# An adaLN transformer block on one core: first modulation in two column halves, E by V in 64x32 tiles, five equal score sets

## The chip, the core and the metric

The kernel runs on one core of a Trainium2 chip. The metric is the device time of one execution in microseconds. Three runs of the kernel before took 323.96, 324.77 and 324.98 us (median 324.77). Beside the times there is one profiled execution, whose trace gives start and duration of every instruction of the engines: PE (matrix engine, with PEld for its weight loads), DVE (vector), ACT (scalar), POOL (GpSimd) and SP, which here only starts transfers.

## The reference

One block of a transformer with adaptive layer norm, for 2048 tokens of width D = 640. A condition vector `c` gives six vectors of length 640, shift, scale and gate for each of two halves of the block.

```python
mod = (silu(c) @ w_mod).reshape(1, 6, 1, 640)        # sa, ca, ga, sb, cb, gb
h = layernorm(x) * (1 + ca) + sa
x = x + ga * attention(h)                            # 32 heads of 20, window of 256 keys, causal
h = layernorm(x) * (1 + cb) + sb
x = x + gb * ((sigmoid(h @ w_gate) * (h @ w_up)) @ w_down)   # inner width 1536
```

Attention: q, k and v are `h @ wqkv`; a query sees itself and the 255 keys before it; softmax over the scores times 20**-0.5; then `@ wo`.

## The kernel before

The 2048 tokens are worked on in eight chunks of 256 (`a` = 0 to 7), each of two blocks of 128 (`bi`). All weights lie in SBUF after the first quarter of the kernel. For every chunk:

- `ln1` (line 897): load, statistics on DVE (line 793), the power -1/2 on POOL (lines 800 and 802), scaling of the block (line 815), turning to columns-by-tokens (PE for chunks 0 and 1, a transposing DMA after that), and the modulation by shift and scale (line 839 and near).
- `qkv` (line 936): Q, K and V projections on PE, five steps of 128 rows each, 320 columns at a time. Each result is copied out of PSUM by ACT or DVE. Q and K are then turned again so that a head's 20 elements lie on partitions: four heads side by side, at partitions 0, 32, 64 and 96. This is done on PE (`NPQ` = 2: chunks 0 and 1) or by a transposing DMA (`transp_dma`).
- `attention` (line 1187): for each half `q` of the heads (16 heads) a chunk sees four blocks of keys. The scores of 16 heads come in sets of 128 x 2048 in PSUM. There is one PSUM tile for a set (`p_S`, four banks), so ACT must have taken the exponential of one set (1.88 us) before PE writes the next. In chunks 1 to 7 there are four main sets (`main_set`, 64-key by 32-row tiles, eight side by side) and one set for the ends of the window (`ends_set`, 128-key tiles, four side by side). POOL zeroes what lies outside the window with affine selections: four for a main set, two for an ends set. Chunk 0 has three sets (`score_set`).
- `burst` (line 1119): E by V for the 16 heads, in 128x32 tiles: all 128 keys of a block at a time, four heads side by side. V has two columns of ones beside each head, so the sum for the softmax comes with the product. The burst of one half is issued in front of the second score set of the next half (`AFTER` = 1), as one operation with it. `norm` then turns the result on DVE, divides and turns back.
- `outproj` and `mlp`: projection by `wo`, residual, second layer norm, gate and up projections, tanh on ACT, product on DVE, down projection, residual, store.

The small products take PSUM from a pool of four banks (`p_M`), shared by all projections, bursts and turnings; a bank is free again once ACT or DVE has read it.

The start is a stage of its own. The weights of the first modulation (`wm0`, 640 x 1280) come in five transfers of 128 rows; five groups of ten 64-column matmuls (`fnA`) follow their arrival, with filler matmuls between (`fill`) and one copy into `mA` (line 778) at the end, for which every modulation of chunk 0 (lines 831 and 832) waits. The first projection is Q of block 0.

The order of all engines is fixed ahead. `PLAN` is a list of 2097 codes, one for each operation: the operation's number times five plus its engine (0 PE, 1 ACT, 2 DVE, 3 POOL, 4 SP). Each engine issues its operations in that order; `schedule` only derives buffers, and `emit` the semaphore waits. Operations that may go to one of several engines (copies out of PSUM, modulations, scalings) have theirs from the list. All matmuls but the smallest are issued from one helper, lines 698 (whole array) and 699 (tiles).

Of the kernel before, what the change touches and what calls it, by code (L numbers as in the profile page):

```python
# [8 lines left out]
ALU = mybir.AluOpType  # L9
# [351 lines left out]
def c_pe(n):  # L361
# [114 lines left out]
]  # L476
NPH = 2
NPQ = 2
PQ = ()
KEEP = 3  # L480
DSAFE = 0.2
# [13 lines left out]
FILL = 1  # L495
WSE = (("dve", "pool"), ("dve", "pool"))
QMAX = 4.5
NE = 6
EW = 2048
PAIR = 0  # L500
PAIRO = 0
# [4 lines left out]
def build(nc, A_x, A_wqkv, A_wo, B_x, B_w_gate, B_w_up, B_w_down, c, w_mod, out, S=2048):  # L506
# [260 lines left out]
    for kt in range(NDT):  # L767
# [7 lines left out]
        if kt:  # L775
            fills.append(fill(FILL, oA[-1:]))
# [611 lines left out]
```

## Time and profile before

| | |
|---|---|
| runs | 323.96, 324.77, 324.98 us |
| span of the profiled execution | 321.8 us, 11465 instructions |
| its own time | not listed apart from the runs; their median is 3.0 us above the span |
| PE busy | 315.6 us (98%), 5045 matmuls |
| PEld busy | 236.8 us (74%) |
| ACT busy | 213.9 us (66%) |
| DVE busy | 198.8 us (62%) |
| POOL busy | 189.5 us (59%) |

Busy times are unions: overlapping matmuls count once, and a matmul's listed duration holds its way through the array, so a group's mean is longer than the distance from one matmul to the next. The chain of waits goes back from the last instruction to what released each step. In its rows a count such as x64 is the number of merged instructions.

### The profile page before, as it was taken

What the parts mean: (1) busy time and instruction counts of PE and PEld (TensorE: products, weight loads), DVE (VectorE), ACT (ScalarE), POOL (GpSimd) and SP (SyncE); (2) the same over time, 40 slices, a digit from 0 to 9 for tenths busy, and PEclk for the clock granted to TensorE, in tenths of its full rate; (3) what the DMA queues carried; (4) which work ended last, traced back from release to release, by engine and by line L of the source; (5) the groups of instructions that cost most, each with busy time, mean ns of one, the idle gap of its engine ahead of it and who ended that gap; (6) DMA issues with size and microseconds to landing.
All of it is one profiled execution on the core that took longest, in us unless ns stands there. A gap on an engine that the chain in (4) does not pass through costs nothing.

```text
span 321.8 us, 11465 instructions
## 1 busy us (share of the span) xinstructions
PE 315.6 (98%) x5045; PEld 236.8 (74%) x5045; DVE 198.8 (62%) x424; ACT 213.9 (66%) x229; POOL 189.5 (59%) x349
## 2 busy tenths in 40 slices
PE   6999999999999999999999999999999999999996
PEld 2677767677877777766777677877877777877885
DVE  4689987877886746584555555465534474386323
ACT  2699997877787986768686867676976746411220
POOL 3338759878768493949484848577575826601000
PEclk9999999999999999999999999999999999999999
DMA  7999999999922534126526100220800004002101
GB/s 249 348 262 278 223 179 248 194 225 295 206 36 43 88 75 55 44 63 108 77 19 111 37 22 2 63 42 25 132 18 4 22 22 104 20 5 61 43 0 41
DMA packets 62123, 32.92 MB, mean 102 GB/s; under 512 B 45946, under 2 KB 60794, under 8 KB 62074
## 3 DMA queue, kind: packets, MB, share of 16 engines
q1 hardware_dynamic: 59904, 29.73, 43.5%
q10 hardware_dynamic: 2170, 2.46, 2.8%
q8 instruction: 39, 0.64, 0.9%
q14 instruction: 10, 0.08, 0.1%
HBM read 18.68 MB, written 2.62 MB: 66 GB/s over the span
## 4 chain that ended last, share of the span: by engine, by line
PE 96%; DMA 1%; DVE 1%; ACT 1%; issue 0%; ACTq 0%
PE M L698 79%; PE S L699 8%; PE M L699 7%; DMA x<-in_A_x_dram 1%; ACT hT L831 1%; DVE st L793 1%; PE S L698 1%; PE S L690 0%; ACT stg L914 0%; ACTq L584 0%; DVE x L815 0%; DVE st L795 0%; ACT hT L914 0%; DVE x L1308 0%; DVE mA L778 0%
## 5 line engine op out<-in xcount | busy, mean ns | idle before, releaser
L1067 ACT ACTIVATE E<-S 128x2048 bf16<-128x2048 f32 x56 | 105.0, 1875 | 40.6 <-PE S L699 40.2
L1072 POOL TENSOR_SCALAR_AFFINE_SELECT E<-E 128x256 bf16<-128x256 bf16 x112 | 46.6, 427 | 57.1 <-ACT E L1067 25.1
L1076 POOL TENSOR_SCALAR_AFFINE_SELECT E<-E 128x512 bf16<-128x512 bf16 x112 | 70.6, 646 | 4.6 <-DVE x L815 1.2
L698 PE MATMUL M<-h2T,wg 128*128 128x256 bf16 x480 | 67.0, 273 | 0.0
L698 PE MATMUL M<-h2T,wu 128*128 128x256 bf16 x480 | 66.7, 273 | 0.0
L1289 DVE SCALAR_TENSOR_TENSOR hh<-sig,M 128x512 bf16<-128x512 f32 x48 | 32.4, 678 | 42.9 <-ACT sig L1287 26.4
L698 PE MATMUL M<-wd,hh 128*128 128x320 bf16 (+2 forms) x396 | 57.1, 295 | 0.0
L698 PEld LDWEIGHTS M<-h2T,wg 128*128 128x128 bf16 x480 | 45.4, 98 | 7.8 <-DVE T L1162 0.2
L698 PEld LDWEIGHTS M<-h2T,wu 128*128 128x128 bf16 x480 | 45.2, 98 | 7.3
L1287 ACT ACTIVATE sig<-M 128x512 f32<-128x512 f32 x48 | 28.5, 595 | 31.2 <-PE M L698 30.9
L698 PEld LDWEIGHTS M<-wd,hh 128*128 128x128 bf16 x396 | 37.2, 98 | 13.7 <-DVE hh L1289 0.2
L1045 POOL TENSOR_SCALAR_AFFINE_SELECT E<-E 128x1024 bf16<-128x1024 bf16 x28 | 32.0, 1147 | 4.9 <-ACT E L1041 3.4
L699 PEld LDWEIGHTS S<-QT,KT 20*64 20x64 bf16 (+1 forms) x1856 | 20.0, 100 | 17.4 <-issue 9.7
L699 PE MATMUL S<-QT,KT 20*64 20x256 bf16 (+5 forms) x1856 | 32.3, 228 | 0.4 <-issue 0.4
L1041 ACT ACTIVATE E<-S 128x2048 bf16<-128x2048 f32 x14 | 26.3, 1876 | 6.8 <-PE S L699 6.7
L793 DVE BATCH_NORM_STATS2 st<-x 128x6 f32<-128x320 bf16 x64 | 28.9, 479 | 2.4 <-DMA x<-in_A_x_dram 1.8
L1162 DVE STREAM_TRANSPOSE T<-M 128x512 f32<-128x512 f32 x32 | 21.5, 700 | 12.9 <-PE S L699 11.6
L698 PE MATMUL M<-wk,hT 128*128 128x320 bf16 x160 | 27.9, 299 | 0.0
L1308 DVE TENSOR_TENSOR x<-M,x 128x320 bf16<-128x320 f32 (+2 forms) x33 | 15.4, 475 | 18.8 <-PE M L698 18.6
L698 PE MATMUL M<-wq,hT 128*128 128x320 bf16 x160 | 26.2, 299 | 0.7 <-DVE hT L832 0.5
L698 PE MATMUL M<-wv,hT 128*128 128x320 bf16 x160 | 26.0, 299 | 0.0
L698 PE MATMUL M<-wo,oT 128*128 128x320 bf16 x160 | 25.9, 299 | 0.0
(84 smaller groups left out, 356.4 us busy)
## 6 DMA issues: line engine op xcount, KB each, us to landing
x<-in_A_x_dram SPq DMA_DIRECT2D x18, 160.0 KB, 3.7
wd<-in_w_mod_dram SPq DMA_DIRECT2D x6, 320.0 KB, 5.4
wd<-in_B_w_down_dram SPq DMA_DIRECT2D x4, 480.0 KB, 5.5
wu<-in_w_mod_dram SPq DMA_DIRECT2D x5, 320.0 KB, 4.8
x<-in_A_x_dram ACTq DMA_DIRECT2D x8, 160.0 KB, 2.7
out_dram<-x SPq DMA_DIRECT2D x8, 160.0 KB, 1.9
wu<-in_B_w_up_dram SPq DMA_DIRECT2D x2, 576.0 KB, 4.7
wg<-in_B_w_gate_dram SPq DMA_DIRECT2D x2, 576.0 KB, 6.8
```

Source lines behind the costliest of these rows:

```text
L698: return e.matmul(o, l, r, start=st, stop=sp, skip_group_check=True)
L699: return e.matmul(o, l, r, start=st, stop=sp, tile_position=tp, skip_group_check=True)
L793: A("dve", lambda e, g, bi=bi, j=j: e.bn_stats(v(bi * 12 + j * 6, 6), src[bi].ap[:, j * 320:(j + 1) * 320]), 0.48, reads=[src[bi].r()], wr ...
L1041: A("act", lambda e, eng: e.activation(cell().rearrange("p m (x c) -> p m x c", c=64)[:, :, 0:4:3, :], Sp.ap[:].rearrange("p j (k x c) -> ...
L1045: A("pool", lambda e, eng, c0=c0, pat=pat, base=base, cm=cm: e.affine_select(cell()[:, :, c0:c0 + 64], cell()[:, :, c0:c0 + 64], pattern=p ...
L1067: A("act", lambda e, eng: e.activation(part(0, 512), Sp.ap[:], ACT.Exp, scale=SM_SCALE), 1.876, reads=[Sp.r()], writes=[E.r("C"), E.r("B") ...
L1072: A("pool", lambda e, eng, hc=hc, src=src, far_h=far_h: e.affine_select(side(hc), part(src, 64), pattern=[[0, 4], [-1 if far_h else 1, 64] ...
L1076: A("pool", lambda e, eng, c0=c0, near=near: e.affine_select(part(c0, 128), part(c0, 128), pattern=[[0, 4], [1 if near else -1, 128]], com ...
L1162: A("dve", lambda e, g, h=h: e.transpose(T1.ap[:, 512 * h:512 * h + 512], X[h].ap), 0.694, reads=[X[h].r()], writes=[T1.r(h)], prio=3.5, t ...
L1287: A("act", lambda e, g, pg=pg, sg=sg: e.activation(sg.ap[:], pg.ap[:], ACT.Tanh, scale=0.5), c_act(512), reads=[pg.r()], writes=[sg.r()], ...
L1289: A("dve", lambda e, g, pu=pu, sg=sg, f0=f0: e.scalar_tensor_tensor(out=hh.ap[:, f0:f0 + 2, :], in0=sg.ap[:].rearrange("p (a b) -> p a b", ...
L1308: A("dve", lambda e, g, ps=ps, bi=bi, c0=c0, n=n: e.tensor_tensor(x1[bi].ap[:, c0:c0 + n], ps.ap[:, 0:n], x1[bi].ap[:, c0:c0 + n], op=ALU. ...
```

## The change

- **First modulation.** `wm0` is loaded in two column halves, columns 0 to 383 and 384 to 639 of each of shift and scale (`CUT` = 3 steps of 128), the first of them in two row parts. The matmuls for the first half are issued for all five steps first, then copied to `mA`; the second half follows with a copy of its own. A modulation or evacuation waits only for the half it reads. The copy of `c` (`c_col`) goes; tanh reads PSUM. `wq` comes in two transfers of its whole width, and the new order starts with the transfer of half of `wk`; the first projection is K of block 1.
- **Score sets.** Every half of the heads in chunks 1 to 7 has five sets of the same form, all in 32x64 tiles with eight side by side: two of two 256-column pieces, two of pieces of 192, 64, 64 and 192 columns, one of four 128-column pieces. Chunk 0 has five sets in all instead of six. The pool `G` for the ends goes, and there are eight E buffers instead of six.
- **Masks.** DVE takes the minimum of E and a constant mask `mk` (0 or 3e38, bf16): one operation per set, 512 or 1024 elements a partition. No affine selection is left on POOL.
- **E by V** in 64x32 tiles, eight side by side: 64 keys of 16 heads, the upper 64 partitions for one group of heads and the lower for the other. Each tile runs the sixteen pieces in the order of `LENS`. V is laid out for this: its projection reads `wv` in runs of 40 columns, and its result is copied out in pieces of 64 partitions, four for each block where there were two of 128.
- **Chunk 1.** `NPQ` = 1 and `PQ`: Q and K of block 0 of chunk 1 are turned by DMA, those of block 1 still on PE.
- **Layer norm** multiplies by r and adds -m*r, with two small POOL operations more (all but the first); the scaling may go to DVE or POOL.
- **The plan** is new: 1977 codes.

```diff
-NPQ = 2
-PQ = ()
+NPQ = 1
+CUT = 3
+PQ = ((1, "q", 1), (1, "k", 1))
...
-NE = 6
+NE = 8
...
-            for t0, t1 in ((0, 3), (3, 5)):
-                dma(lambda t0=t0, t1=t1: W3[k][:, t0:t1, 0:320], lambda t0=t0, t1=t1: wqkv_src[:, t0:t1, 0:320], 0.224 * (t1 - t0),
+            for t0, t1 in ((0, CUT), (CUT, NDT)):
+                dma(lambda t0=t0, t1=t1: W3[k][:, t0:t1, :], lambda t0=t0, t1=t1: wqkv_src[:, t0:t1, 0:D], 0.448 * (t1 - t0),
...
-    load_bulk(wm_ap[0], wm_src[:, :, 0:1280], Rm[0], 0.88, 0.2, "wm0", dlat=2.89)
+    for part, (lo, hi) in enumerate(((0, 128 * CUT), (128 * CUT, D))):
+        k = 0
+        for m in (3, 5) if part == 0 else (5,):
+            for b in (1, 0):
+                dma(lambda k=k, m=m, lo=lo, hi=hi, b=b: wm_ap[0][:, k:m, b * D + lo:b * D + hi],
...
+    for part, (lo, hi) in enumerate(SPAN):
+        n = (hi - lo) * MW
+        for kt in range(NDT):
+            def fnA(e, g, kt=kt, lo=lo, hi=hi, part=part, n=n):
+                for b in (1, 0):
+                    for cg in range(lo, hi):
+                        ins = mm(e, psA.ap[:, part, b * n + (cg - lo) * MW:b * n + (cg - lo + 1) * MW],
...
+        A("dve", lambda e, g, lo=lo, hi=hi, part=part, n=n: e.tensor_copy(
+            mA[:, :, lo:hi], psA.ap[:, part, 0:2 * n].rearrange("p (b a m) -> p b a m", b=2, m=MW)[:, :, :, 0]), 0.17,
...
+                    wv[:, kt, :].rearrange("p (g c) -> p g c", c=80)[:, :, 40 * half:40 * half + 40])) for kt in range(NDT)]
...
+                for odd in range(2):
+                    evac(lambda b=b, half=half, odd=odd: heads(V[b].ap[64 * half:64 * half + 64, 352 * odd:352 * odd + 352], VW)[:, :, 0:DH],
...
+    ONE = ((-1, 0), (0, 256))
+    TWO = ((-2, 0), (-4, 192), (3, 256), (1, 320))
+    SETS = (([(h, x, c) for x, c in st] for st in (ONE, TWO) for h in range(2)))
+    SETS = [list(x) for x in SETS] + [[(h, x, c + 256 * h) for h in range(2) for x, c in ((-3, 0), (2, 128))]]
+    MASKS = [(192, 512, 4, 128, 64)] * 2 + [(128, 512, 4, 256, 0)] * 2 + [(64, 256, 8, 128, 64)]
+    FIRST = ((1, 0), (3, 192), (0, 256))
...
+            prog = {(j, half): [0] + [(q, h, x, c, piece(x)[3]) for q, h, x, c in parts] for j in range(4) for half in range(2)}
...
+                return mm(e, Sp.ap[64 * half:64 * half + 64, j, c:c + n], keys_of(a, kb, 64 * odd, gi, j, 64),
+                          QT[a].ap[32 * j:32 * j + DH, gi, q0:q0 + n], True, True, tp=(32 * j, 64 * half))
...
+                return e.tensor_tensor(v, v, mk[:, m0:m0 + w].unsqueeze(1).to_broadcast([128, g, w]), op=ALU.min)
...
+    LENS = (64, 256, 192, 192, 128, 128, 192, 256, 128, 128, 192, 256, 256, 64, 64, 64)
+    LENS0 = (64, 192, 256, 256, 128, 128, 192, 64)
...
+                ins = mm(e, X[half].ap[32 * j:32 * j + 32, h * 256 + q0:h * 256 + q0 + n],
+                         V[2 * a + kb].ap[64 * half:64 * half + 64, v0:v0 + 32],
+                         E.ap[64 * half:64 * half + 64, j * 512 + c:j * 512 + c + n], t not in seen, True, tp=(64 * half, 32 * j))
...
+            if not a:
+                sets = [([(q, h, x, c) for x, c in FIRST], [(0, 512, 4, 64, 128), (192, 512, 4, 128, 128)]) for h in range(2)]
+                if q == 0:
+                    sets.append(([(p, h, 2, 256 * p + 128 * h) for p in range(2) for h in range(2)], [(0, 128, 16, 64, 128)]))
```

More of the change, by code (lines that the diff above doesn't have):

```diff
@@ L797, in ln_stats @@
         one = ln == "a" and a == 0
+        if not one:
+            A("pool", lambda e, g: e.tensor_scalar(v(34, n), st.ap[:, 24:28].rearrange("p (b t) -> p b t", t=2)[:, :, 0], -1.0, None,
+                                                   op0=ALU.mult), 0.2,
+              reads=[st.r(("m", bi)) for bi in range(n)], writes=[st.r("g")], prio=1, tag=f"{ln}neg{a}")
         var = lambda: st.ap[:, 24:28].rearrange("p (b t) -> p b t", t=2)[:, :, 1]
@@ L986, in qkv @@
-            if PAIR:
-                evac(lambda b=b: both(heads(V[b].ap[:, 0:H * VW], VW)[:, :, 0:DH]), lambda pss=pss: both_banks(pss), 640,
-                     [ps.r() for ps in pss], [V[b].r(0), V[b].r(1)], 6.5, f"evv{a}")
-    last = {"s": fills, "p": []}
-    def plan(a):
-        if a == 0:
-            return [([(0, 0, 0, 2, 0), (1, 0, 0, 2, 2)], ((0, 2, 2),), ()), ([(2, 0, 0, 2, 0), (3, 0, 0, 2, 2)], ((0, 2, 2),), ()),
-                    ([(k, 1, 1, 1, k) for k in range(4)], ((0, 1, 4),), ())]
-        return [0, 1, None, 2, 3]
+                    ps.ap[:, 0:320].rearrange("p (g c) -> p g c", c=40), hT[a].ap[:, kt, bi * 128:(bi + 1) * 128],
@@ new lines, in qkv @@
+                    wv[:, kt, :].rearrange("p (g c) -> p g c", c=80)[:, :, 40 * half:40 * half + 40])) for kt in range(NDT)]
+                pe_chain(ps, 320, pairs, [R_w3["wv"] + [hT[a].r((kt, bi) if a == 0 else kt)] for kt in range(NDT)], prio, f"projv{a}",
+                         hold=[V[b]])
+                for odd in range(2):
+                    evac(lambda b=b, half=half, odd=odd: heads(V[b].ap[64 * half:64 * half + 64, 352 * odd:352 * odd + 352], VW)[:, :, 0:DH],
+                         lambda ps=ps, odd=odd: heads(ps.ap[64 * odd:64 * odd + 64, 0:320], DH), 320, [ps.r()], [V[b].r((half, odd))], 6.5,
+                         f"evv{a}")
@@ L1001, in with_pv @@
+    last = {"s": fills, "p": []}
     def with_pv(name, sc, dur, rd, tiles, before, mode):
         if before is None:
-            return A("pe", sc, dur, reads=list(rd), writes=[tiles[-1].r()], prio=10, lat=0.2, tag=name, extra=last["s"], mode=mode,
-                     hold=tiles[:-1])
+            return A("pe", sc, dur, reads=list(rd), writes=[t.r() for t in tiles[1:]], prio=10, lat=0.2, tag=name, extra=last["s"], mode=mode,
+                     hold=tiles[:1])
         pa, pv, pd, prd, X = before
@@ L1020, in set_reads @@
         rd = {}
-        for kb in range(-2, 2):
+        for kb in range(-2 if a else 0, 2):
             rd[KT[(2 * a + kb) // 2].r((kb % 2, q))] = 1
@@ L1121, in burst, with run @@
-    def burst(a, q, sets, Es, G):
+    def run(e, prog, emit):
+        at = {t: p[0] for t, p in prog.items()}
+        pos = dict.fromkeys(prog, 1)
+        ins = None
+        while pos:
+            t = min(pos, key=lambda t: (at[t], list(prog).index(t)))
+            what = prog[t][pos[t]]
+            if isinstance(what, int):
+                at[t] = max(at[t], what)
+            else:
+                ins = emit(e, t, what)
+                at[t] += what[-1]
+            pos[t] += 1
+            if pos[t] == len(prog[t]):
+                del pos[t]
+        return ins
@@ new lines, in score_set, with put, fn @@
+    def score_set(a, name, parts, masks, before):
+        E, Sp = Tile(p_E, f"E{a}_{name}"), Tile(p_S, f"S{a}_{name}")
+        def sc(e, eng):
+            prog = {(j, half): [0] + [(q, h, x, c, piece(x)[3]) for q, h, x, c in parts] for j in range(4) for half in range(2)}
+            def put(e, t, what):
+                j, half = t
+                q, h, x, c, n = what
+                kb, odd, q0, n = piece(x)
+                gi = 4 * q + 2 * half + h
+                return mm(e, Sp.ap[64 * half:64 * half + 64, j, c:c + n], keys_of(a, kb, 64 * odd, gi, j, 64),
+                          QT[a].ap[32 * j:32 * j + DH, gi, q0:q0 + n], True, True, tp=(32 * j, 64 * half))
+            return run(e, prog, put)
+        rd = {}
+        for q in dict.fromkeys(x[0] for x in parts):
+            rd.update(set_reads(a, q))
+        last["s"] = [with_pv(f"score{a}", sc, 0.262, rd, [E, Sp], before, 3)]
+        A("act", lambda e, eng: e.activation(E.ap.rearrange("p (j c) -> p j c", j=4), Sp.ap[:], ACT.Exp, scale=SM_SCALE), 1.876,
+          reads=[Sp.r()], writes=[E.r()], prio=3, tag=f"exp{a}")
+        for c0, step, g, w, m0 in masks:
+            def fn(e, eng, c0=c0, step=step, g=g, w=w, m0=m0):
+                v = E.ap.rearrange("p (g c) -> p g c", c=step)[:, :, c0:c0 + w]
+                return e.tensor_tensor(v, v, mk[:, m0:m0 + w].unsqueeze(1).to_broadcast([128, g, w]), op=ALU.min)
+            A("dve", fn, c_dve(g * w, 2.0), port=True, reads=[E.r(), R_mk], writes=[E.r()], prio=5, tag=f"mask{a}")
+        for q, h, x, c in parts:
+            where[a, q, h, x] = E, c
+        return E
@@ L1123, in burst @@
+    XS = {64: (-4, 3), 128: (-3, 2), 192: (-2, 1), 256: (-1, 0)}
+    LENS = (64, 256, 192, 192, 128, 128, 192, 256, 128, 128, 192, 256, 256, 64, 64, 64)
+    LENS0 = (64, 192, 256, 256, 128, 128, 192, 64)
+    where = {}
+    def burst(a, q):
         X = [Tile(p_M, f"O{a}_{q}x"), Tile(p_M, f"O{a}_{q}y")]
         X[0].mate, X[1].mate = X[1], X[0]
+        of = {n: [(h, x) for h in range(2) for x in XS[n] if a or x >= 0] for n in XS}
+        mine = [p + where[(a, q) + p] for p in (of[n].pop(0) for n in (LENS if a else LENS0))]
@@ L1139, in pv @@
-            for (E, _), st in zip(Es, sets) if not a else ():
-                for k, kb, u, n, cu in st[0]:
-                    bank = k // 2
-                    oc = (k % 2) * 256 + u * 128
-                    for j in range(4):
-                        h = 16 * q + 4 * j + k
-                        ins = mm(e, X[bank].ap[32 * j:32 * j + 32, oc:oc + n * 128], V[2 * a + kb].ap[:, h * VW:h * VW + 32],
-                                 E.ap[:, j * 512 + cu * 128:j * 512 + (cu + n) * 128], (bank, j) not in seen, True, tp=(0, 32 * j))
-                        seen.add((bank, j))
@@ L1148, in pv, with put @@
-            return ins
-        rd = {}
-        for E, rs in Es:
-            rd.update(dict.fromkeys(rs))
-        if G is not None:
-            rd.update(dict.fromkeys([G.r("A"), G.r("D")] + [G.r((x, k)) for x in "AD" for k in range(4)]))
+            prog = {(half, j): [0] + [x + (piece(x[1])[3],) for x in mine] for half in range(2) for j in range(4)}
+            def put(e, t, what):
+                half, j = t
+                h, x, E, c, n = what
+                kb, odd, q0, n = piece(x)
+                v0 = (16 * odd + 2 * (4 * q + j) + h) * VW
+                ins = mm(e, X[half].ap[32 * j:32 * j + 32, h * 256 + q0:h * 256 + q0 + n],
+                         V[2 * a + kb].ap[64 * half:64 * half + 64, v0:v0 + 32],
+                         E.ap[64 * half:64 * half + 64, j * 512 + c:j * 512 + c + n], t not in seen, True, tp=(64 * half, 32 * j))
+                seen.add(t)
+                return ins
@@ L1154, in burst @@
+            return run(e, prog, put)
+        rd = {x[2].r(): 1 for x in mine}
         for kb in range(-2 if a else 0, 2):
-            rd[V[2 * a + kb].r(0)] = 1
-            rd[V[2 * a + kb].r(1)] = 1
-        return a, pv, (6 if a else 3) * 512 / 2400.0 * 1.04 + 0.02, rd, X
+            for half in range(2):
+                for odd in range(2):
+                    rd[V[2 * a + kb].r((half, odd))] = 1
+        return a, pv, 1.205 if a else 0.625, rd, X
     def norm(X, Tn, q, a):
@@ L1172, in build, with later @@
     pend = []
-    def later(a, q, sets, Es, G, close):
+    def later(a, q, close):
         made = []
         def first():
-            made.append(burst(a, q, sets, Es, G))
+            made.append(burst(a, q))
             return made[0]
@@ L1215, in attention @@
             if a < NOW:
-                alone(*later(a, q, sets, Es, G, close))
+                alone(*later(a, q, close))
             else:
-                pend.append(later(a, q, sets, Es, G, close))
+                pend.append(later(a, q, close))
     def add_pair(x, pss, prio, tag):
```

250 lines of the change are left out of this document (75 added, 175 removed), and 217 rows, old and new, of the table PLAN.

## The prediction

> **What bounds the kernel now.** I read the page's head and its chain of waits first, then the stretches of the span, then the chain in order of time.
>
> ```profile
> span 321.8 us, 11465 instructions
> PE 315.6 (98%) x5045; PEld 236.8 (74%) x5045; DVE 198.8 (62%) x424; ACT 213.9 (66%) x229; POOL 189.5 (59%) x349
> ...
> PE 96%; DMA 1%; DVE 1%; ACT 1%; issue 0%; ACTq 0%
> ```
>
> ```profile
> 0.00:8.00 8.00, 5.20 (x25) 1.95 (x26) 3.24 (x11) 1.96 (x3) 3.02 (x18) 1.00 0.75 248
> 8.00:16.00 8.00, 7.35 (x97) 5.04 (x93) 4.88 (x15) 4.94 (x12) 3.22 (x9) 1.00 1.10 348
> ...
> 32.00:64.00 32.00, 31.60 (x577) 22.10 (x575) 26.99 (x65) 28.31 (x35) 24.35 (x41) 1.00 1.09 210
> 64.00:96.00 32.00, 32.00 (x568) 24.21 (x565) 25.73 (x56) 23.87 (x24) 23.67 (x42) 1.00 0.93 194
> ```
>
> The columns are PE, PEld, DVE, ACT, POOL, then the granted clock (1.00 throughout), DMA share and GB/s. TensorE is busy without a gap from about 14 us on. A busy PE need not be a fast PE, so I checked its rate:
>
> ```profile
> 129.00 1.80 PE L698 MATMUL M<-wd,hh 128*128 128x320 bf16 x12
> 130.64 0.60 PE L698 MATMUL M<-h2T,wg 128*128 128x256 bf16 x4
> ```
>
> Twelve matmuls of 320 columns pass in 130.64 - 129.00 = 1.64 us: 0.427 ns a column. The long stream at the end (320 matmuls, 37.19 us) has no holes either. So the time is the PE's work plus the start and the tail. An edit that shortens PE work shortens the kernel, and an edit elsewhere counts only if it makes PE wait.
>
> ```profile
> 118.72 2.75 PE M L698 x23
> 121.47 1.43 PE M L699 x64
> 122.90 0.36 PE S L699 x24
> 123.26 2.36 PE M L698 x17
> 125.62 0.34 PE S L699 x32
> ...
> 137.99 1.50 PE M L699 x64
> ...
> 282.24 37.19 PE M L698 x320
> ```
>
> The 64-matmul rows are the bursts that multiply E by V, fourteen for chunks 1 to 7, at 1.43 to 1.50 us. The x24 and x32 rows are score sets. The time of the profiled execution itself is not listed; the median of the runs is 324.77 us, 3.0 us outside the span. I make the sum against span + 3.0, which is that median (runs 323.96 to 324.98).
>
> **E by V in 64x32 tiles.** Before, four tiles of 128x32 each stream 16 pieces, 4 x 768 = 3072 columns: 1.31 us at 0.427, and the rows have 1.43 to 1.50, so 0.12 or more is entry and switch. After, eight tiles each stream 16 pieces, 2560 columns (the sum of LENS): 1.09 us. Entry and switch I take from the score sets: 512 columns are 0.22 us, and the set with eight tiles takes 0.36, the one with four 0.34, so eight tiles cost 0.02 more. That gives 1.09 + 0.12 + 0.02 = 1.23 us if the weight loads, now 128 a burst, stay hidden. If each load-and-matmul pair needs what the x32 row shows, 0.22 us / 32 = 7 ns, a group of eight 64-column pieces takes 56 ns instead of 27; there are four such groups: +0.12, so 1.35 us. I take 1.28, a little under the middle since the score sets show no such cost, against a mean of 1.45 in the chain: **-0.17 x 14 = -2.4 us** (ends -1.4 and -3.1).
>
> **Score sets.** Chunks 1 to 7 keep five sets of 512 columns per half of the heads. The ends set goes from 0.34 to the 0.36 of eight tiles: 14 x 0.02 = **+0.2** (rounded down). Chunk 0 goes from six sets to five and its two E-by-V bursts from 4 x 384 to 1280 columns.
>
> ```profile
> 18.18 0.33 PE S L699 x8
> ...
> 29.32 0.72 PE M L699 x33
> ```
>
> 6 x 0.33 becomes 5 x 0.36 (-0.2), and the bursts lose 256 columns each (-0.11 x 2): **-0.4**.
>
> **Chunk 1 turned by DMA.** NPQ 2 to 1 with PQ leaves block 1 of chunk 1 on PE and sends Q and K of block 0 through two transposing DMAs more. Four groups of four 128-column matmuls go: 16 x 128 x 0.427 ns = **-0.9 us**, hidden by nothing, since PE is full there. Their four copies out of PSUM go too. The DMAs join SP's queue where the DMA share is 1.09; what is late if they are slow is chunk 1's first score set, and PE then needs other projections ahead of it.
>
> **The start.** Loads, PE and DVE meet here.
>
> ```profile
> GB/s 0 0 29 278 348 316 318 355 376 362 395 363 364 378 369 369 318 289 324 326 360 345 273 319 246 111 150 347 229 300 353 254 314 300 280 336 313 335 309 287
> ...
> wd<-in_w_mod_dram SPq DMA_DIRECT2D x5, 320.0 KB, 5.6
> ```
>
> ```profile
> 9.66 1.13 PE L698 MATMUL S<-silubc,wd 128*128 128x64 bf16 x30
> 10.83 0.17 DVE L778 COPY mA<-S 128x10 f32<-128x10 f32 x1 [1.46 <-PE S L698]
> 11.71 2.06 PE L698 MATMUL M<-wq,hT 128*128 128x320 bf16 x14 [0.49 <-DVE hT L832]
> 13.94 0.57 PE L698 MATMUL M<-wq,hT 128*128 128x320 bf16 x3 [0.16 <-ACT stg L914]
> ```
>
> The first row has 40 slices of 0.75 us over the first 30 us; the second is the first modulation's weights. Before, 246 KB of wq, two x blocks (328) and 1638 KB of modulation weights, 2.21 MB, have moved by 8.6 us; the copy of the modulation comes at 10.83, behind 30 matmuls at 0.033 us each. After, the new order issues wk's first half (410) and the last columns of one operand (328) ahead, then x and the first columns (983): the first half is complete at 2.05 MB, 8.2 us, 0.4 earlier, and its copy stands behind 30 matmuls instead of 50, 0.6 earlier: a copy at 9.8. Against that, the other 20 matmuls (0.65 us) and a second copy stand before the first projections in PE's new order and before all but the first three of their five steps, and x block 0 now lands behind 738 KB of SP's queue, 1.3 us later (block 1 goes through ACT's queue and is turned first). wq now waits behind wk: 3.44 MB, 12.0 us; eight K chains of 5 x 0.137 us cover it. The ends are +0.5, if block 0's late chain is not covered, and -1.0; I take **-0.5**, nearer the gain because the copy itself has rows for it.
>
> **Masks on DVE, POOL emptied.** The 258 POOL selections (the costliest group below) go; 79 DVE minima with a mask come.
>
> ```profile
> L1076 POOL TENSOR_SCALAR_AFFINE_SELECT E<-E 128x512 bf16<-128x512 bf16 x112 | 70.6, 646 | 4.6 <-DVE x L815 1.2
> L815 DVE TENSOR_SCALAR x<-x,st 128x640 bf16<-128x640 bf16 x26 | 11.2, 446 | 8.6 <-POOL st L802 8.4
> L915 DVE CAST V<-M 128x320 bf16<-128x320 f32 x23 | 10.9, 478 | 7.7 <-PE M L698 7.5
> L1308 DVE TENSOR_TENSOR x<-M,x 128x320 bf16<-128x320 f32 x31 | 14.8, 485 | 17.3 <-PE M L698 17.1
> L1333 DVE TENSOR_TENSOR wo<-wo,gbc 128x640 bf16<-128x640 bf16 x5 | 2.1, 486 | 0.0
> ```
>
> Nearest row, both operands bf16 in SBUF: 486 ns for 640, 0.76 ns an element. Each half of a chunk's heads masks 2 x 512 + 3 x 1024 = 4096 elements, 3.1 us; with chunk 0 fifteen such, 46.7 us. A code of the plan is five times the operation plus its engine, so the diff also says who does what: DVE goes from 424 operations to 489, POOL from 337 to 147, ACT from 244 to 239. V is evacuated in 64 pieces instead of 32, 32 of them on DVE (23 before, +4.3 us); sixteen of the 26 scalings of row L815 move to POOL (-7.1); eight weight scalings too (-4). DVE comes to some 238 us, 74% of the span, and stands beside PE. In 32 to 64 us, with four such halves in about 64 us, it is 27.0 + 6.2 - 4 or so: full, but not over. Cost nothing in the sum; without the moved work 1 to 3 us.
>
> [...]
>
> **Instruction blocks.** A burst with its score set goes from 176 instructions (a load and a matmul each) to 288.
>
> ```profile
> q8 instruction: 39, 0.64, 0.9%
> ```
>
> 0.64 MB for 10,090 PE instructions is 64 bytes each, 256 to a packet; 0.9% of 16 x 321.8 us over 39 packets is 1.2 us a packet. A burst that crosses two edges uses up a whole block in about 1.3 us, hardly more than a packet takes. Counting two instructions a matmul through the new plan, bursts begin at places 16 to 248 of a block, two of fourteen in its last 32 (the count leaves waits out, so its zero is uncertain). Between 0 and two packets, 2.4, I take **+0.4**.
>
> **Sum:** -2.4 + 0.2 - 0.4 - 0.9 - 0.5 + 0.4 = -3.6: span 318.2, **time 321.2 us**. Own range 319.6 to 322.8.
>
> **Rivals.**
>
> Half the gain. The start is bound by x and the second modulation half, so nothing is won there, the loads take the 7 ns (-1.4) and each of the two edges costs a packet (+2.4 less the 0.4 counted). Two of these three give 322.5 to 323.5; say **323.0**. For it: the start's PE work before the second copy is the same. Against: the score sets' eight tiles run at their columns.
>
> DVE bounds the first 96 us. If the masks run at row L1308's 1.5 ns, 32 to 96 us holds 52.7 + 4 x 6.2 = 77 us in 64; the plan's moves take back some 9, so about 4 us come back on PE, since the V and projection copies queue behind the masks and free PE's banks: 321.2 + 3.6 = **324.8**, no change. For it: DVE and ACT are already at 84 and 88% there. Against: row L1333.
>
> Slower: PE's instructions do not arrive fast enough. The place is each burst. The trace shows 64 instructions in 0.34 us (5.3 ns each) but over 176 no better than 1.79 us (10.2 ns), where the columns set the pace. The new burst and set need 288 in 1.64 (5.7 ns). From 6.3 ns (1.81 / 288) a burst gains nothing; at 8 it takes 2.30, +0.49 x 14 = 6.9 in place of -2.4, so with the other edits (-1.6) **330**; at 10.2 ns 339. For it: no long run at the needed rate is in the trace. Against: nothing in the bursts of before shows a hole.
>
> [...]
>
> **How the numbers follow.** Forecast 0.60, half the gain 0.14, DVE 0.11, supply 0.15. A measurement of this kernel tells about 0.3%, 1 us, from no change. Faster by more: 0.60 + 0.14 = 0.74; within: 0.11; slower: 0.15. The range goes from the own low end with all bounds good (318.9) to past the DVE case (325.4); what is left out is the supply case and a little.
>
> **What would show it.** The x64 bursts become x128 at 1.23 to 1.35 us; over 1.45 shows supply or loads. Every score set at 0.36. Copies of mA at about 9.8 and 11.2, the first projection ahead of 11.7. Masks at 0.39 and 0.78 us on DVE, POOL near 75 us busy. PE without gaps after 14 us; gaps before M whose releaser is DVE would show the second rival, gaps in a burst that name no engine ("issue") the third. The prediction is wrong if PE loses more than 2 us to any of these, or if the burst is no shorter.

## The result, and the profile after

| | before | after |
|---|---|---|
| runs beside each other, median | 324.37 us (323.42 to 324.98, 4 runs) | 333.56 us (332.93 to 333.72, 4 runs) |
| ratio | | 1.0298 [1.0263, 1.0333] |
| span of the profiled execution | 321.8 us | 331.6 us |
| matmuls | 5045 | 6054 |

The change makes the kernel 9.2 us slower; 3.6 us less were forecast. Head of the page, its queue of instructions and the shares of the chain, after:

```profile
span 331.6 us, 13379 instructions
PE 316.1 (95%) x6054; PEld 233.5 (70%) x6054; DVE 231.5 (70%) x492; ACT 211.9 (64%) x231; POOL 79.8 (24%) x160
q8 instruction: 47, 0.77, 1.0%
PE 84%; ACT 5%; DVE 5%; issue 2%; DMA 1%; SPq 0%; DVEq 0%
```

PE is as busy as before in us, but no longer the whole chain. The stretches (columns as before: PE, PEld, DVE, ACT, POOL, granted clock, DMA share, GB/s) say where:

```profile
8.00:11.00 3.00, 3.00 (x37) 2.24 (x35) 1.41 (x4) 0.23 (x1) 0.80 (x4) 0.50 1.15 326
...
32.00:64.00 32.00, 28.04 (x702) 18.75 (x703) 27.18 (x62) 26.28 (x33) 15.52 (x30) 1.00 1.05 214
64.00:96.00 32.00, 29.29 (x686) 21.01 (x684) 26.36 (x57) 25.06 (x27) 9.85 (x17) 1.00 0.87 162
```

In 32 to 96 us PE stands still for 6.7 us where it had stood for 0.4. At 8 to 11 us the granted clock is 0.50, which it never was before. What PE waited for, from the table of waits (total us, times, longest):

```profile
PE M L716 <- issue: 2.7, 4, 0.7
PE M L716 <- DVE x L838: 2.2, 1, 2.2
PE M L717 <- issue: 2.1, 1, 2.1
PE M L717 <- DVE E L1090: 1.4, 2, 1.2
PE S L717 <- issue: 1.3, 1, 1.3
...
PE M L716 <- ACT V L938: 0.9, 1, 0.9
```

The three rows "issue" are 6.1 us in six holes for which the profile names no engine; before, that row was one hole of 0.4 us. In the chain in order of time four of the six are:

```profile
47.78 0.73 issue
...
58.72 1.26 issue
...
86.71 1.37 PE M L717 x104
88.08 2.08 issue
90.16 0.25 PE M L717 x15
...
204.91 1.30 PE M L717 x121
206.21 0.35 PE S L717 x16
206.56 1.41 PE M L716 x10
207.97 0.73 issue
```

The largest stands inside a burst, after 113 of its 128 matmuls by the timeline. A burst without a hole takes 1.30 us (x121 at 204.91); 1.28 was forecast. In the records of the instruction queue, packets end at 35.37, 47.24, 58.37 and 88.84 us, and PE goes on 1.2 to 1.6 us after each; the other two of the six holes follow a packet by 1.42 us. One ends at 41.40 too, 1.35 us ahead of the end of the hole that the table puts to ACT's copy of V (the last row). That hole stands 126 matmuls behind the first of the six and 127 ahead of the second, so it is probably a seventh. And the one hole of before, 0.4 us until 42.85, follows a packet that ended at 41.47. I also added up, for all matmuls, the distance from one start to the next less what that matmul takes: holes over 0.15 us come to 3.7 us before and 15.9 after, and all the rest is 2.4 us shorter: 15.9 - 3.7 - 2.4 = 9.8, the difference of the spans. So the shorter work is there, and holes eat it five times over. Not all are holes without a name: those, with the seventh, are some 7 us of the 12.2 us more, and the rest are waits for masks, at the start, and small ones.

### The profile page after: what moved, and what is told of

Read it like the earlier page. It is cut to its first block, busy times and chain, and to the rows that moved or that the text cites. A ratio compares the mean times of both kernels' runs of the same rounds, so it can differ in the third digit from the quotient of the medians.

```text
span 331.6 us, 13379 instructions
## 1 busy us (share of the span) xinstructions
PE 316.1 (95%) x6054; PEld 233.5 (70%) x6054; DVE 231.5 (70%) x492; ACT 211.9 (64%) x231; POOL 79.8 (24%) x160
## 4 chain that ended last, share of the span: by engine, by line
PE 84%; ACT 5%; DVE 5%; issue 2%; DMA 1%; SPq 0%; DVEq 0%
PE M L716 69%; PE S L717 8%; PE M L717 7%; ACT E L1085 5%; DMA x<-in_A_x_dram 1%; DVE E L1090 1%; DVE V L939 1%; DVE st L817 1%; PE S L716 1%; DVE stg L939 1%; PE S L708 1%; ACT V L938 0%; DVE hh L1256 0%; DVE QT L939 0%; SPq L582 0%
## 5 line engine op out<-in xcount | busy, mean ns | idle before, releaser
L1085 ACT ACTIVATE E<-S 128x2048 bf16<-128x2048 f32 x75 | 140.8, 1877 | 48.0 <-PE S L717 47.2
L716 PE MATMUL M<-h2T,wu 128*128 128x256 bf16 x480 | 68.2, 273 | 0.1
L1090 DVE TENSOR_TENSOR E<-E,mk 128x1024 bf16<-128x1024 bf16 (+2 forms) x79 | 43.3, 557 | 8.0 <-ACT E L1085 7.8
L717 PE MATMUL S<-QT,KT 20*64 20x64 bf16 (+3 forms) x1920 | 32.6, 236 | 1.7 <-issue 1.3
L716 PE MATMUL M<-wq,hT 128*128 128x320 bf16 x160 | 28.0, 300 | 1.6 <-ACT V L938 0.9
L717 PEld LDWEIGHTS S<-QT,KT 20*64 20x64 bf16 x1920 | 17.0, 104 | 17.4 <-ACT E L1085 6.9
L716 PE MATMUL M<-wv,hT 128*128 128x320 bf16 x160 | 27.4, 299 | 1.4 <-issue 1.3
L864 POOL TENSOR_SCALAR h2T<-h2T,scB,shB 128x256 bf16<-128x256 bf16 x19 | 10.8, 576 | 65.4 <-DVE h2T L864 27.8
L839 POOL TENSOR_SCALAR x<-x,st 128x640 bf16<-128x640 bf16 x22 | 19.2, 876 | 23.6 <-DVE E L1090 15.5
L717 PEld LDWEIGHTS M<-E,V 64*32 64x32 bf16 x1920 | 19.3, 90 | 7.0 <-issue 3.8
```

Of the source, the lines that this page charges most:

```text
L716: return e.matmul(o, l, r, start=st, stop=sp, skip_group_check=True)
L717: return e.matmul(o, l, r, start=st, stop=sp, tile_position=tp, skip_group_check=True)
L839: return e.tensor_scalar(dst[bi].ap[:], src[bi].ap[:], v(30 + bi, 1), v(32 + bi, 1), op0=ALU.mult, op1=ALU.add)
L864: return e.tensor_scalar(ap, ap, sc[:, dt:dt + 1], sh[:, dt:dt + 1], op0=ALU.mult, op1=ALU.add)
L1085: A("act", lambda e, eng: e.activation(E.ap.rearrange("p (j c) -> p j c", j=4), Sp.ap[:], ACT.Exp, scale=SM_SCALE), 1.876, reads=[Sp.r()], ...
L1090: return e.tensor_tensor(v, v, mk[:, m0:m0 + w].unsqueeze(1).to_broadcast([128, g, w]), op=ALU.min)
```

## The experiments

Theory: the holes are PE out of instructions. The page has 0.77 MB in 47 packets of the instruction queue, 16 KB each; at two instructions a matmul that is 64 bytes an instruction, so by this estimate a packet holds 256 of them, called a block here. A block that is used up in a few us would be over before the next is there. Rivals: DVE, which now holds the masks; ScalarE; the clock at the start; or the order of the plan.

**More instructions, in the kernel before.** Each piece of E by V is cut in two; columns, tiles and plan stay.

```diff
-                    for j in range(4):
-                        src = ... E.ap[:, j * 512 + c0:j * 512 + c0 + n]
+                    for part in range(2):
+                        m = n // 2
+                        for j in range(4):
+                            base = (4 * j + k) * 256 + c0 if side else j * 512 + c0
+                            src = (G if side else E).ap[:, base + part * m:base + part * m + m]
```

> The kernel before, with each E-by-V piece of chunks 1 to 7 issued as two matmuls of half its columns: the same 3072 columns a tile, 128 matmuls a burst instead of 64, masks, sets and start untouched. Theory A (PE's instructions come in blocks of 256 and a block needs 3.6 to 4 us from its request, more beside bulk transfers; 304 instructions in 1.8 us run ahead of it): gaps of 0.8 to 2.2 us that name no engine, at block ends, in the bursts that begin near 244, 14, 240 and 198 of a block; 4 to 8 us in all, so 328.5 to 332.5. Theory B (the new time lies in DVE's masks and evacuations, or in the tiles' form): only 16 x 2.5 ns a burst more, +0.6, 325.

Measured: 341.26 us, ratio 1.0523 [1.0476, 1.0570]. In the chain, and in the stretches behind the first hole:

```profile
54.13 3.15 issue
57.28 0.63 PE S L699 x16
57.92 3.37 PE M L698 x15
```

```profile
57.00:60.40 3.40, 3.12 (x28) 1.88 (x28) 2.09 (x4) 1.88 (x1) 1.92 (x5) 0.50 0.85 180
60.40:64.00 3.60, 3.60 (x78) 2.34 (x75) 2.75 (x10) 2.21 (x2) 1.87 (x4) 1.00 0.39 73
```

Nothing but the number of instructions has changed, and four holes of 1.9 to 3.15 us appear, with a small fifth 10.7 in all. Each of the four is followed by 3.4 us at half clock, in which about 1.7 us of work (half of the 3.4) are lost: 10.7 + 4 x 1.7 = 17.5, and the kernel is 17.8 slower. The forecast, at most 332.5, had 4 to 8 us of holes and no half clock.

**Fewer instructions, in the kernel after.** Half of each burst's pieces are left out, the others have 320 columns: the columns stay, a burst has 64 matmuls.

```diff
-            prog = {(half, j): [0] + [x + (piece(x[1])[3],) for x in mine] ...}
+            prog = {(half, j): [0] + [x + (i, 320) for i, x in enumerate(mine[::2])] ...}
```

> The changed kernel, in which each E-by-V tile runs 8 pieces of 320 columns instead of 16 of mixed length: the same 2560 columns, 64 matmuls a burst instead of 128. Half of the keys' pieces are left out of the product and the others read past their end, so the attention output is not the reference's. Everything else, masks and sets too, is the same. Theory A: the gaps in the bursts go (4.0 us) and some of the four early ones (4.1 us): 326 to 329.5. Theory B: 333, no change.

Measured: 326.31 us, 1.0095 [1.0059, 1.0130], 7.2 us less than after (6.6 by the ratios, since before was measured anew beside it). Of the holes without a name 0.6 us are left, and a burst takes 1.21 us to the next matmul. 5.5 us of holes and 14 x 0.09 us of bursts make 6.8. But this kernel, with shorter bursts than the forecast's, is still slower than before; the rest of the experiments but one are about that.

**Edges shifted.** Nine matmuls more in PE's idle stretch at 5.5 to 7.8 us move every later block edge by 18 instructions, once with 64 columns and once with 512, which also fills the stretch.

```diff
+    def padfn(e, g):
+        for k in range(9):
+            ins = e.matmul(p_S.aps[0][:, 3, 0:64], Eall[:, 0:128], Eall[:, 128:192], start=True, stop=True)
+        return ins
```

> The changed kernel with nine 64-column matmuls more on zeros, in PE's idle time before the first turning (5.5 to 7.7 us). They shift every later block end by 18 instructions. Theory A: the 2.25 us gap inside the burst at 88 us goes (its burst begins at place 40 of a block instead of 22), those at 106.9 and 208.7 stay or grow to about 1.2 (211 and 220 instead of 193 and 202), the early ones move by nine matmuls: 331.5 to 333. If the gaps belong to the places in the program and not to the block ends, they stay at the same matmuls and the time is 333.5.

> The same nine matmuls with 512 columns each, so the block ends lie as in the run with nine small ones, and PE is busy from 5.5 to 7.7 us. If the half clock granted from 7.7 to 11.1 us in the changed kernel comes of that idle time, the clock stays at 1.0, the copies of mA come 0.7 to 1.5 us earlier and the time is 0.5 to 1.5 us under that run. If the start is bound by the loads, no change.

Measured: 338.75 us (1.0463 [1.0431, 1.0496]) and 337.91 us (1.0406 [1.0351, 1.0461]). The holes moved with the edges. The one inside the burst now stands after 104 of its matmuls, where it had stood after 113: nine earlier, as nine were added. In the first run:

```profile
86.75 1.34 PE L717 MATMUL M<-E,V 64*32 64x64 bf16 x104
89.48 0.28 PE L717 MATMUL M<-E,V 64*32 64x64 bf16 x24 [1.38 <-issue]
```

The hole in the score set at 60 us likewise comes after 2 of its 32 matmuls instead of 11. So in these runs holes belong to counts of instructions and not to places of the program. Their sizes were not foreseen: the one in the burst was to go and went from 2.08 to 1.38 us in both, others grew to 1.53 (41 us) and 1.75 (208 us) in the first. Its three rows "issue" come to 6.5 us, and behind the hole at 208 it ran 3.4 us at half clock. In the second the rows are 4.7 us and the clock is 1.00 throughout, but PE waits for other things there (the transposes on DVE 1.4 us, the tanh 1.0, the load of `wv` 0.9), and its four runs spread from 335 to 340. The second is 0.8 us under the first, as the clock's theory had it, but their intervals overlap. Both are slower than forecast, and not all of that is placed.

**The disputed cost by itself.** Into the last part of the kernel before, where DMA is quiet, goes one run of 768 small matmuls, 1536 instructions, whose result is not used.

```diff
+        for k in range(96):
+            for half in range(2):
+                for j in range(4):
+                    ins = mm(e, Sp.ap[32 * j:32 * j + 32, half, 0:64], ident[64 * half:64 * half + 64, 0:32],
+                             ident[64 * half:64 * half + 64, 0:64], True, True, tp=(64 * half, 32 * j))
```

> The kernel before with one run of 768 added matmuls (64 rows by 32 columns of weights, 64 columns, eight tiles) in the last part, where DMA is quiet; the result is not used. 1536 instructions are six blocks of 256. Theory: a block of instructions takes 3.6 to 4 us to come, however fast the ones before it are used up; one or two blocks are there already, so the run takes 15 to 22 us, with a hole in PE every 128 matmuls. Rival: the instructions' own rate is the limit: at the 5.3 ns of a score set's instruction 8.1 us, without holes; by columns alone 2.6 us.

Measured: 345.93 us, 1.0697 [1.0637, 1.0757]. PE's timeline and one stretch (granted clock third from the end):

```profile
295.73 2.13 PE L588 MATMUL S<-ident 64*32 64x64 bf16 x221
300.04 1.22 PE L588 MATMUL S<-ident 64*32 64x64 bf16 x128 [2.18 <-issue]
304.04 1.28 PE L588 MATMUL S<-ident 64*32 64x64 bf16 x128 [2.79 <-issue]
307.77 1.28 PE L588 MATMUL S<-ident 64*32 64x64 bf16 x128 [2.45 <-issue]
311.50 1.28 PE L588 MATMUL S<-ident 64*32 64x64 bf16 x128 [2.45 <-issue]
315.23 0.50 PE L588 MATMUL S<-ident 64*32 64x64 bf16 x35 [2.45 <-issue]
```

```profile
302.00:304.00 2.00, 0.00 (x0) 0.00 (x0) 0.00 (x0) 0.00 (x0) 0.00 (x0) 0.50 0.00 0
```

This is the cost laid bare. Exactly 128 matmuls, 256 instructions, pass between two holes, and blocks follow each other every 3.73 us (307.77, 311.50, 315.23), of which PE needs 1.28. The run takes 315.73 - 295.73 = 20.0 us. The instructions' own rate, 8.1 us, is not the limit. So in this run the next block came after 3.73 us even where the DMA share was 0.00 to 0.03 (298 to 316 us). The half clock in that stretch does not set it: in the changed kernel, at 1.00, the two holes behind 96 us end 3.8 and 3.6 us after the block before began (counting 127 matmuls a block), which was used up in 3.1 and 2.9. No block there that lasted 3.8 us or more ends in a hole without a name. The packet is only a third of the 3.73: the last three packets start 1.0 to 1.1 us after a block begins, take 1.15 to 1.3, and PE goes on 1.4 to 1.5 after their end.

Four of the six holes lie in the first 96 us, beside the loads. There the next block came 5.0 to 5.8 us after the one before, and blocks used up in 3.5 to 5.0 us were too short. Those packets take no longer (1.0 to 1.1 us); they start later, 2.3 to 3.4 us after the block begins.

**DVE's masks.** On top of the half pieces, each mask is cut to two columns of its group, so most scores outside the window are not put to zero.

```diff
+                w = 2
```

> The changed kernel with half the pieces of each E-by-V burst (64 matmuls of 320 columns a tile in place of 128 mixed ones; the other products are left out) and with each mask cut to 2 columns of its group, so that scores outside the window are mostly not put to zero. Compared with the same kernel with full masks (326.3). Theory: DVE's 43 us of masks, as a load on DVE, make the small waits of PE (V, projections, score sets) that eat the gain of the shorter bursts. Then the masks' time falls to about 10 us and the kernel comes 2 to 3 us lower, 323.3 to 324.3. Rival: ScalarE's exponentials, not DVE, set those waits; then at most 0.5 lower, 325.8 to 326.3.

Measured: 325.95 us, 1.0083 [1.0057, 1.0109], 0.4 under the same kernel with full masks (1.0095). DVE's busy time falls from 231.9 to 203.0 us. Taken alone, the masks are not what keeps PE, as the rival said; the next pair of runs limits that.

**The clock at the start.** Nine matmuls of 512 columns in the idle stretch, without and with the light masks.

> The changed kernel with half the pieces of each burst (the rest left out) and nine added matmuls of 512 columns in PE's idle stretch after the first transposes, whose result is not used. With half the pieces alone the granted clock was 0.5 from 8.05 to 11.47 us. Theory: PE's idle time before it halves the clock, and that costs 1.0 to 1.7 us; with the added matmuls the clock stays at 1.00 and the time is 324.6 to 325.3. Rival: loads bind the start, the clock costs nothing: 326.3.

> Half the pieces of each burst, masks of 2 columns and the nine added matmuls together (the products and the zeroing left out as in the two others). Theory: instruction supply, the clock at the start and DVE's load are the three places where the forecast gain went; with all three taken away 321.5 to 323.3, near the forecast of 321.2. Rival: something else remains (ScalarE's exponentials, the order of the plan): 324.5 or more.

Measured: 325.57 us (three runs, 1.0079 [1.0050, 1.0109], none with a trace) and 324.02 us (1.0024 [1.0008, 1.0040]). By the ratios the added matmuls alone gave 0.5 us where 1.0 to 1.7 were expected, the light masks alone 0.4, and both together 2.3. So the two do not add up: beside the added matmuls light masks are worth 1.8 us, and DVE's load is not free there. Why is not settled; the added matmuls also move every block edge. That the half clock costs little fits the runs without these matmuls: with light masks 325.44 to 326.09 us at a mean granted clock of 0.995 and 326.27 at 1.00, with full masks 326.08 to 328.26 at 0.995 and 325.98 and 326.31 at 1.00. The kernel with all three has a clock of 1.00 throughout and no long holes, and it is still no faster than before. Between its trace and that of before, by start-to-start distances: bursts -3.2 us, turns by PE -0.95; against that the Q, K and V projections +2.3 and the modulations +0.5. The gain does arrive on PE and is then spent waiting.

The same question without added instructions: six filling matmuls move ahead into the idle stretch of the whole changed kernel.

```diff
-        o = A("pe", fn, 0.2154 * n, prio=-1000, reads=[R_z], extra=extra + wprev, tag="fill", writes=[R("w")])
+        o = A("pe", fn, 0.2154 * n, prio=-1000, reads=[R_z], extra=wprev, tag="fill", writes=[R("w")])
```

> The changed kernel with the same instructions: only the six filling matmuls between the first modulation's steps (512 columns, 0.22 us each) move ahead into PE's idle stretch after the first transposes, so every block of 256 instructions after 13 us keeps its edges. Theory: the half clock from 7.7 to 11.1 us follows from that idle stretch (2.25 us) and costs 1.0 to 1.7; with 0.95 us idle the clock stays at 1.00, and the ratio to before falls from 1.030 to 1.025 to 1.027. Rival: the loads set the start; then 1.030 again.

Measured: 333.79 us, 1.0317 [1.0276, 1.0357]: nothing won. The half clock is gone in the profiled execution (333.87 us; 18 of the 64-column matmuls pass in 0.69 us where 12 took 0.80), though the three other runs have a mean of 0.995 like the changed kernel's and the same time. The first projection starts at 11.10 us instead of 12.48, and every burst is 0.6 to 1.2 us earlier, the last at 274.41 instead of 275.19. Then comes this, in the chain:

```profile
275.04 3.88 DMA out_dram<-x
278.92 0.02 issue
278.94 0.37 ACTq L474
279.31 0.05 issue
279.36 0.61 ACT sig L1146
279.96 0.05 issue
280.01 5.12 PE M L608 x38
```

ACT's queue waits for a store of the output, the tanh of the gate stands behind it, and PE waits 1.0 us for the tanh. The time fits the rival, but not by its cause: of the 1.4 us won at the first projection, some 0.6 went to waits before 60 us, as for the load of `wv` at 20 us, and the rest to a queue 220 us later.

**ScalarE's exponentials.** On top of the kernel with all three taken away, the exponentials from the ninth on take 336 of 512 columns, so a third of the scores is left out there.

```diff
-        ... e.activation(E.ap.rearrange("p (j c) -> p j c", j=4), Sp.ap[:], ACT.Exp, scale=SM_SCALE), 1.876,
+        ... e.activation(E.ap.rearrange("p (j c) -> p j c", j=4)[:, :, 0:wx], Sp.ap[:, :, 0:wx], ACT.Exp, scale=SM_SCALE), 1.3,
```

> The kernel of half pieces, masks of 2 columns and nine added matmuls, and now ScalarE's exponentials too are cut: from the ninth on, 336 of each 512 columns (so 34% of those scores are never turned into weights). With full exponentials it took 324.0. Theory: what is left after instruction supply, the clock and DVE's load are PE's short waits ahead of score sets and bursts for ScalarE's exponentials, about 2 us. Then 321.5 to 322.5. Rival: these waits come from the plan's order or from loads; then 323.5 to 324.0.

Measured: 327.31 us, 1.0103 [1.0062, 1.0143], that is 3.3 slower than with full exponentials (2.6 by the ratios). Neither theory had that. The chain has

```profile
43.11 1.05 issue
...
56.42 0.91 issue
...
63.15 0.59 issue
...
268.34 4.29 DMA out_dram<-x
...
273.07 0.60 ACT sig L1261
273.73 2.40 PE M L716 x18
```

PE's short waits ahead of score sets did fall, from 1.7 to 0.1 us in all (distance to the set beyond the usual one), so ScalarE had made those. But at block edges there are now three holes, 2.55 us, where the kernel with full exponentials has none over 0.35. PE did not come to these edges earlier (43.11 us against 42.86 at the first, and later at the other two); the packet came later (its end 42.85 against 41.64), and why is not settled. The queue of ACT behind the output store takes 1.6 us more. Whether ScalarE's waits would pay once blocks are in time was not tried.

**One part alone: chunk 1 turned by DMA,** in the kernel before, Q and K of block 0, then K alone (`NPQ` and `PQ` as below, for K alone with `(1, "q", 0)` in `PQ` too; the turns and copies leave the plan, the transfers stand behind the copy they need).

```diff
-NPQ = 2
-PQ = ()
+NPQ = 1
+PQ = ((1, "q", 1), (1, "k", 1))
```

> The kernel before with one part of the change alone: Q and K of block 0 of chunk 1 are turned by two DMAs in place of sixteen matmuls and four copies; nothing else moves. The term of the sum was -0.9 us: 323.4 to 323.8 against a before of 324.5. Rival: chunk 1's score sets then wait for the late transposes and PE has nothing to put in their place: 0 to +1 us.

> The kernel before with K alone of block 0 of chunk 1 turned by a DMA (eight matmuls and two copies fewer); Q's turn, whose DMA came 3.1 us late, stays on PE. The term is half of -0.9: 0.45 us faster. Rival: the turning DMA holds up the loads behind it on SP's queue, and PE waits later (two waits of 1.3 and 0.8 us at 68 and 80 us with both turned): 0 to 2 us slower.

Measured: 327.01 us (1.0123 [1.0079, 1.0167]) and 324.73 us (1.0029 [0.9999, 1.0058]). First the chain of the kernel with both, then the waits of that with K alone:

```profile
29.32 5.95 DMA QT<-stg
35.27 0.25 issue
35.51 0.43 PE S L588 x17
```

```profile
PE M L587 <- issue: 2.1, 1, 2.1
PE M L588 <- issue: 1.5, 1, 1.5
```

The transposing transfer of Q takes 5.95 us beside the loads, and chunk 1's first score set waits 3.0 us for it: the rival's place, at more than the rival's price. Behind the wait the granted clock is 0.50 for 3.4 us (thirteen matmuls of 320 columns take 3.33 us there, 0.26 each, against 0.137). With K alone that wait goes, but two holes without a name come in the profiled execution (327.24 us, among the slowest of ten), 3.6 us. The later one, until 77.07, follows a packet that ended at 75.71, as the holes above do; ahead of the earlier one's end at 38.23 no packet had ended for 4.7 us, so that one is left open. The runs spread from 323.3 to 327.6, and a gain of 0.45 cannot be told. None of the versions tried beats the kernel before.

## Why the prediction was wrong

**The step that failed is "Instruction blocks".** It took a packet's own 1.2 us for what a block costs, put the ends at 0 and 2.4 and chose +0.4. Measured are 6.1 us in six holes (5.7 more than before). What counted was the time from block to block, 3.73 us in the long run with DMA quiet and 5.0 to 5.8 at the holes of the changed kernel beside the loads. The blocks of before lasted 8 us each on average (321.8 / 39), so its trace shows little of it; but it does hold one such hole, 0.4 us in the middle of a score set, and I passed over that. The places of bursts in their blocks, which the term counted, shift a hole and its size (2.08 to 1.38 us, 0.73 to 1.75); whether there was one hung, in the changed kernel, on how fast a block was used up (2.9 and 3.1 us behind 96 us, 3.5 to 5.0 beside the loads). The upper end should have been left open: the term said itself that a burst uses up a block in 1.3 us, hardly more than a packet takes. The step is about half of the miss of 12.8 us: almost without holes, and with bursts of 1.21 us, the kernel of half pieces is still 2.8 us slower than the before beside it, where 3.6 less were forecast.

**The third rival was right in its cause and in half its size, and wrong in its mechanism.** It forecast 330, 5.2 us slower, by slower bursts; 9.2 came, with bursts of 1.30 us and holes. Its sign, a gap without a name inside a burst, came once. In the long run PE took 5 ns an instruction as long as the block was there (1.28 us for 256). Its chance of 0.15 was too small: "no long run at the needed rate is in the trace" was all it had for it, and a missing row is no evidence against.

**Bursts:** forecast 1.28 us, measured 1.30, term -2.4 against about -1.8 (14 x (1.43 - 1.30), by distances from start to start; the forecast's 1.45 took durations). **Score sets:** 0.35 to 0.37, as forecast (206.21 above). **Chunk 1 turned by DMA:** by start-to-start distances the turns fall from 3.92 to 2.97 us (in the kernel of half pieces), the forecast 0.9. In the new order no row of the waits names these two transfers; in the old one they cost 3.8. **Chunk 0:** forecast -0.4. Its five sets take 0.36 each, which is the -0.2 of the sets; the bursts gave nothing, 0.71 us against 0.72 although they have 256 columns fewer each. Here the mixed short pieces gained less than their columns.

**The start** was wrong in sign. The `mA` copies were to come at 9.8 and 11.2 and the first projection before 11.7:

```profile
1.80 4.43 DMA x<-in_A_x_dram
6.23 0.02 issue
6.26 0.90 DVE st L817 x2
```

```profile
11.34 0.17 DVE L801 COPY mA<-S 128x6 f32<-128x6 f32 x1 [1.50 <-PE S L716]
```

The chain ends its wait for x at 6.23 us, the case of the bound +0.5. PE has nothing to do until 7.76, the half clock follows, and the second copy comes at 12.68, the projection at 12.48 against 11.71: +0.8 instead of -0.5. What that costs in the end is small, as the moved fills show: time won at the start is lost again at a load or a queue.

**Masks on DVE** were sized rightly:

```profile
L1090 DVE TENSOR_TENSOR E<-E,mk 128x1024 bf16<-128x1024 bf16 x43 | 29.0, 682 | 7.0 <-ACT E L1085 7.0
...
L1090 DVE TENSOR_TENSOR E<-E,mk 128x512 bf16<-128x512 bf16 x32 | 13.5, 423 | 1.0 <-ACT E L1085 0.8
```

0.42 and 0.68 us against 0.39 and 0.78, DVE 231.5 us against 238, POOL 79.8 against 75. "Cost nothing" was too little: PE waits 1.4 us in all for masks, and light masks gave back 0.4 us alone and 1.8 beside the added matmuls. The second rival falls as it was put: its 1.5 ns an element did not come, nor its 4 us.

**The sum's frame failed too.** "An edit that shortens PE work shortens the kernel" holds while PE is the only bound. With all three suspects taken away the kernel is 0.8 us slower than the before measured beside it, where 3.6 less were forecast: about 4.4 us go elsewhere, into waits of 0.1 to 0.5 us as far as the trace shows. Some are for ScalarE (1.7 us ahead of score sets, where before has 0.3), the others are not settled one by one.

**Bounds.** The ends of the terms do not add up to the range: all good they give 319.6 and not 318.9, all bad 325.2. Two of the three losses of the first rival give 322.7 to 324.2. None of this reaches 333.6.

## What to carry to other kernels

Count instructions per 256, not only columns. In the changed kernel PE stood still where it had used up 256 in 2.9 and 3.1 us behind the loads, or in 3.5 to 5.0 us beside them, and in the long run, from its first hole on, it stood still after every 256, used up in 1.28 us. So look, before tiles are made smaller, how fast the instructions they add will be used up. Measure the supply by itself with one long run of tiny matmuls before building on a higher rate. And when the bound engine gets faster by one per cent, price the next wait at every place where it meets another engine, since those places were tuned to the old pace.

## What the runs showed of the hardware that was not expected

- In the long run of small matmuls, from the first hole on, PE stood still after every 128 matmuls, 256 instructions. It needed 1.22 to 1.28 us for them and began the next 3.73 us after these (4.00 the first time), with a DMA share of 0.00 to 0.03. In the traces of before and of the changed kernel a packet of the instruction queue took 0.9 to 1.6 us. At four holes of the changed kernel beside bulk loads PE went on 5.0 to 5.8 us after the block before had begun, and the packets started 2.3 to 3.4 us into that block.
- After PE stood still, its granted clock was at times 0.50 for 3.4 us. In the kernel before with pieces cut in two it was so from 57.0, 80.9, 169.6 and 190.1 us on, each time after PE had stood still (four holes of 1.9 to 3.15 us). The length of a hole alone did not tell: in the run with nine small matmuls the clock was 0.50 from 211.1 to 214.5 us, behind the hole of 1.75 us at 208, and in the changed kernel it stayed at 1.00 from 88 to 96 us, behind the one of 2.08 us at 88. What decides between the two was not shown.
- A transposing transfer of one block took 5.95 us beside bulk loads in the kernel before; in the changed kernel the median of the thirteen of Q is 4.5 us from issue to landing, of the thirteen of K 4.1.
